# Slots 4 to 7 turned by TensorE, and the first two FFN tiles by whole products

## The chip, the cores and the metric

One core of one Trainium2 chip runs the whole program. The time is device time in microseconds of one execution. The program is one launch: attention for 64 heads, then a feed-forward block over its output, in fp32.

## The reference, cut to what matters

```python
# attention: q, k, v of shape (8, 8, 576, 64), tau = 0.02
scores = scale * q @ k.T
scores = np.where(scores >= max(scores) - tau, scores, -1e9)
attn = np.exp(scores - max(scores))
attn = attn / (np.sum(attn, -1) + 1e-9)
x = (attn @ v) as (8 * 576, 8 * 64)              # 4608 tokens x 512
# FFN: w_in (512, 1024), w_out (1024, 512), g_ln (1024,); the weights come as float64
h = x @ w_in
solu = h * softmax(h)
ln = (solu - mean) / np.sqrt(var + 1e-6) * g_ln
out = ln @ w_out                                 # (4608, 512)
```

## The kernel before, in words

**Slots and rounds.** The work is a list of 144 slots, 18 for each of the 8 batches. A slot `(b, kind, hp, r)` is one 128-row block of scores for two heads: for kinds 0 and 1, `hp` names one of four pairs of heads and `r` one of two row blocks, and slots come in twos (r = 0 and 1) that form a *unit*; the last two slots of a batch (kind 2) gather the 64 rows that are left of every head. A loop goes through rounds, one slot per round, and goes on behind the last slot until the FFN is done. What each engine does in a round is written out by hand (`tc.manual_schedule()`), and every engine works through its own instructions in the order in which the program text issues them. So the order in the text is the order in the queue.

**One slot.** `scores` puts the products of the two heads into two PSUM tiles s0 and s1 (128x576 of 128x1024 each). `maxes` finds each row's threshold on VectorE (L455), `ramp` applies it on ScalarE (L470), `exps` takes the exponentials and their sums on ScalarE (L479). One round later `normalise` forms 1/(sum + 1e-9) on GpSimd (L486, L487) and multiplies both blocks by it there (L489). `blocks` then transposes 32x32 blocks on VectorE (L501), and when both slots of a unit are there, three DMAs (L510, L512) move groups of 32 partitions so that the keys lie on the partitions (tile `wT`). All DMAs but one are issued by SyncE's queue.

**The attention product.** `attend_steps` multiplies a unit's `wT` by v with 64x64 products (L542; an fp32 product is two TensorE instructions, so 72 per unit); `attended` copies the result into the token tile `xh` on ScalarE (L572). The list `pv_due` says in which round a unit's product is due: three rounds behind its second slot, four for some early ones. Products, FFN tiles and other short uses share two PSUM tiles of 128x1024, p0 and p1, which `take` hands out and which return to `pairs_free`.

**The FFN.** A tile of 128 tokens goes through `ff_h` (hidden product in two halves, L605, 64x64 products with a fence in between), `ff_max`, `ff_exp`, `ff_mul`, `ff_sum`, `ff_stats`, `ff_norm` (ScalarE, V), `ff_norm2` (VectorE), `ff_swap` (four DMAs), `ff_turn` (32x32 transposes, L697), `ff_o` (output product, two halves, L710), `ff_out` and `ff_store`. The variables `cur`, `prev` and `quarter` walk through this in quarters, one per round. The first tiles, (0,0,0) and (0,0,1), can begin when the four units of kind 0 of batch 0 have their products.

**The first 16 rounds** also convert the weights from float64 to fp32, one piece of 128x512 per round: `weight_e` on ScalarE (L263), `weight_m` on VectorE (L282 and L286), `weight_b` on VectorE (L308), `weight_c` on GpSimd (L332), and for w_out `weight_f`, a multiplication by the gain on ScalarE (L340). `weight_d` (L347) then copies halves of two pieces of w2 to other partitions by two DMAs. The pieces are loaded by `weight_load` some rounds ahead.

## Time and profile before

| | before |
|---|---|
| median of 3 runs | 860.53 us (854.51 to 861.35) |
| span of the profiled execution | 854.9 us, 36109 instructions |
| TensorE busy, products | 819.9 us (96%) |
| VectorE busy | 674.6 us (79%) |
| ScalarE busy | 570.0 us (67%) |
| GpSimd busy | 496.1 us (58%) |
| DMA, moved | 168.54 MB, 197 GB/s on average |

The profiled execution is one of its own, beside the three runs; the profile gives its span from the first to the last instruction and no other time for it. The span lies 0.4 us above the lowest of the three runs and 5.6 below their median. Busy times count what an engine's instructions take, without its queue's waiting. In rows of the trace the engines are PE (TensorE), PEld (its weight loads), DVE (VectorE), ACT (ScalarE), POOL (GpSimd) and SP (SyncE); a row of the order of time gives the start in us, the length in us, engine, line, operation, what it writes and reads, and how many instructions are joined in it; behind it in brackets stands the idle time ahead and what ended it. A row of a group gives busy us and the mean in ns.

### The profile page before, as it was taken

To read this page: it belongs to the slowest core of one execution; us is meant where nothing else is said; L and a number is where in the kernel's file an instruction comes from. 1 tells how busy PE (TensorE), PEld (TensorE's weight loads), DVE (VectorE), ACT (ScalarE), POOL (GpSimd) and SP (SyncE) were. 2 spreads that over 40 slices of the span, in tenths; PEclk is the share of its full clock that TensorE was granted. 3 is DMA by queue.
4 is the path that set the end of the run, shared out by engine and by line. 5 is a ranking of instruction groups with operands and counts; after the bars stand their busy time and mean duration, and the time that the engine had idled before them with its cause. 6 is when DMAs were issued, how large, how long until landed. Compare 5 with 4: busy or idle time off the path is not lost.

```text
span 854.9 us, 36109 instructions
## 1 busy us (share of the span) xinstructions
PE 819.9 (96%) x15363; PEld 620.5 (73%) x15363; DVE 674.6 (79%) x1225; ACT 570.0 (67%) x1127; POOL 496.1 (58%) x945
## 2 busy tenths in 40 slices
PE   6778899999999999999999999999999999999997
PEld 5555677778677787777688877777777777777655
DVE  5997787989788888888788878888888878787361
ACT  6886876777767666667666666666677777775121
POOL 4885656666566656565566666565666655555120
PEclk8899999999999999999999999999999999999999
DMA  9999778798888888887888778887788887655212
GB/s 343 254 249 213 191 194 233 188 259 204 226 229 202 211 185 218 216 216 190 201 215 218 195 177 209 207 217 207 195 221 226 207 188 175 165 137 140 67 38 63
DMA packets 75314, 168.54 MB, mean 197 GB/s; under 512 B 11146, under 2 KB 32658, under 8 KB 75154
## 3 DMA queue, kind: packets, MB, share of 16 engines
q1 hardware_dynamic: 74866, 165.82, 76.7%
q8 instruction: 120, 1.97, 1.0%
q10 hardware_dynamic: 288, 0.43, 0.2%
q14 instruction: 40, 0.33, 0.1%
HBM read 46.14 MB, written 9.44 MB: 65 GB/s over the span
## 4 chain that ended last, share of the span: by engine, by line
PE 83%; DMA 4%; DVE 4%; ACT 3%; issue 2%; POOL 2%; SPq 1%; DVEq 0%; ACTq 0%; POOLq 0%
PE o_ps L710 27%; PE h_ps L605 22%; PE s_ps L434 15%; PE pv L542 14%; DMA wT<-T 3%; PE h_ps L595 3%; ACT w L470 1%; DVE w L455 1%; ACT w L479 1%; DVE T L501 1%; POOL w L489 1%; POOL sm L487 0%; PE s_ps L379 0%; DVE w L308 0%; PE tp L371 0%
## 5 line engine op out<-in xcount | busy, mean ns | idle before, releaser
L710 PE MATMUL o_ps<-w,uT 64*64 64x256 f32 x4608 | 269.5, 376 | 2.2 <-issue 1.6
L470 ACT ACTIVATE w<-s_ps,nth 128x576 f32<-128x576 f32 x280 | 196.8, 738 | 105.6 <-DVE nth L455 88.6
L455 DVE CUSTOM_DVE_ANT_0 w<-s_ps,tau_t 128x576 f32<-128x576 f32 x280 | 200.0, 751 | 83.5 <-PE s_ps L434 52.4
L710 PEld LDWEIGHTS o_ps<-w,uT 64*64 64x64 f32 x4608 | 221.8, 133 | 55.4 <-ACT xh L572 12.0
L489 POOL TENSOR_SCALAR w<-w,sm 128x576 f32<-128x576 f32 x288 | 220.6, 778 | 14.3
L501 DVE STREAM_TRANSPOSE T<-w 128x576 f32<-128x576 f32 x288 | 207.7, 756 | 22.6 <-POOL w L489 22.3
L605 PE MATMUL h_ps<-w,xh 64*64 64x512 f32 x1856 | 220.8, 589 | 0.0
L479 ACT ACTIVATE w<-w,ntau 128x576 f32<-128x576 f32 x288 | 219.6, 767 | 0.0
L542 PEld LDWEIGHTS pv<-wT,v 64*64 64x64 f32 x5760 | 172.6, 136 | 39.8 <-issue 16.7
L434 PE MATMUL s_ps<-kT,qT 64*64 64x512 f32 (+1 forms) x2048 | 175.8, 416 | 13.4 <-ACT w L470 11.3
L542 PE MATMUL pv<-wT,v 64*64 64x128 f32 (+1 forms) x5760 | 173.9, 263 | 8.3 <-DMA wT<-T 7.4
L605 PEld LDWEIGHTS h_ps<-w,xh 64*64 64x64 f32 x1856 | 118.4, 133 | 77.2 <-issue 43.6
L486 POOL TENSOR_SCALAR sm<-sm 128x2 f32<-128x2 f32 x144 | 34.2, 237 | 186.5 <-ACT w L479 182.8
L487 POOL TENSOR_TENSOR sm<-sm,mone 128x2 f32<-128x2 f32 x144 | 106.7, 741 | 12.0
L434 PEld LDWEIGHTS s_ps<-kT,qT 64*64 64x64 f32 x2048 | 72.7, 137 | 21.7 <-ACT w L470 16.2
L572 ACT COPY xh<-pv 128x256 f32<-128x256 f32 x64 | 25.4, 396 | 80.9 <-PE pv L542 80.9
L671 ACT ACTIVATE V<-u,nb,rs 128x1024 f32<-128x1024 f32 x36 | 44.7, 1240 | 40.5 <-POOL nb L661 33.6
L697 DVE STREAM_TRANSPOSE uT<-V 128x1024 f32<-128x1024 f32 x36 | 44.1, 1225 | 15.9 <-DMA V<-u 15.6
L479 ACT ACTIVATION_READ_ACCUMULATOR w<-w,ntau 128x1 f32 x288 | 55.4, 192 | 0.0
L676 DVE TENSOR_SCALAR u<-u,rs,nb 128x1024 f32<-128x1024 f32 x36 | 34.9, 971 | 19.5 <-ACT V L671 17.9
L635 DVE TENSOR_TENSOR u<-h_ps,u 128x1024 f32<-128x1024 f32 x36 | 42.8, 1190 | 9.4 <-ACT u L629 9.4
L620 DVE TENSOR_REDUCE hm<-h_ps 128x1 f32<-128x1024 f32 x36 | 42.9, 1193 | 4.9 <-PE h_ps L595 2.7
(77 smaller groups left out, 553.5 us busy)
## 6 DMA issues: line engine op xcount, KB each, us to landing
wT<-T SPq DMA_DIRECT2D x160, 288.0 KB, 6.5
wT<-T SPq DMA_DIRECT2D x64, 576.0 KB, 5.5
v<-in_v_dram SPq DMA_DIRECT2D x16, 576.0 KB, 6.0
V<-u SPq DMA_DIRECT2D x144, 64.0 KB, 3.5
out_dram<-ob SPq DMA_DIRECT2D x71, 128.0 KB, 2.6
q<-in_q_dram SPq DMA_DIRECT2D x28, 288.0 KB, 6.1
k<-in_k_dram SPq DMA_DIRECT2D x27, 288.0 KB, 6.4
qT<-flip SPq DMA_DIRECT2D x48, 144.0 KB, 3.2
```

What stands on the lines that cost most here:

```text
L434: nc.tensor.matmul(out=ps[h][ROWS[y], ks], lhsT=lhsT, rhs=d["kT"][ROWS[h], ks], start=True, stop=True,)
L455: nc.vector.tensor_tensor_reduce(out=w, in0=ps[:, 0:S], in1=(zero if loose else tau_t).to_broadcast([P, S]), scale=1.0, scalar=BIG, op0=AL ...
L470: nc.scalar.activation(out=d["w"][x], in_=d["w"][x] if d["loose"] else d["ps"][x][:, 0:S], func=AF.Prelu, bias=d["nth"][x], scale=-1.0, al ...
L479: nc.scalar.activation(out=w, in_=w, func=AF.Exp, bias=ntau, scale=1.0, accum_out=sm[:, x : x + 1])
L487: nc.gpsimd.tensor_tensor(out=sm, in0=sm, in1=mone, op=ALU.pow)
L489: nc.gpsimd.tensor_scalar(out=w, in0=w, scalar1=sm[:, x : x + 1], scalar2=1.0, op0=ALU.mult, op1=ALU.mult)
L501: nc.vector.transpose(out=T[:, :, r, h, :], in_=w)
L542: nc.tensor.matmul(out=to, lhsT=d["v"][ROWS[u], (h0 + h - u) % 4, m,], rhs=rhs, start=m == 0, stop=m == NK - 1,)
L605: mm = nc.tensor.matmul(out=h[ROWS[y], f], lhsT=x[ROWS[r], c, ROWS[y]], rhs=w1_parts[ROWS[r], c, part ^ r], start=part == 0 and c == 0, st ...
L671: nc.scalar.activation(out=V, in_=u, func=AF.Identity, bias=nb, scale=rs)
L697: nc.vector.transpose(out=uT, in_=d["V"].rearrange("p y (m x) -> p m y x", x=32))
L710: nc.tensor.matmul(out=d["o"][ROWS[z], 512 * (r ^ other) : 512 * (r ^ other) + 256], lhsT=d["uT"][ROWS[r], m].rearrange("p y x -> p (y x)" ...
```

## The change

Slots 4 to 7 (two units, kind 0, the third and fourth pair of heads) are no longer turned by VectorE and DMAs. `flip` turns the exponentials by 128x128 transposes on TensorE: four full blocks per head into one PSUM tile (`room`), the last 64 columns into a corner of a second one (`extra`). ScalarE copies the corner (`keep_rest`), VectorE the rest (`keep_flip`). These slots are not multiplied by 1/sum; `attend_flipped` spreads 1/sum over the rows by a product with the identity, ScalarE copies that to SBUF, and `attended_flipped` multiplies behind the product with v. For that v of these heads is loaded in another order (`load_moved_v`), and in batch 0 the keys lie in their natural order.

The inverse of sums is formed on VectorE for slots 4 to 17 and for the FFN in rounds 4 to 17 (`inverse`). The first step of a weight's conversion, L282, goes to GpSimd for pieces 4 and later (`weight_s`), the gain (`weight_f`) from ScalarE to GpSimd, and the copies of `weight_d` to rounds 13, 15, 17 and 19.

A table, `STEPS`, says for rounds 5 to 18 which attention product ("a"), which quarter of a hidden product ("c"), which turning of u ("x") and which half of an output product ("o") TensorE does. The first two FFN tiles use whole 128x128 products and are turned by TensorE (`ff_flip`), so `ff_norm2`, `ff_swap` and `ff_turn` fall away for them. From round 19 on the old walk goes on, with the second tile's output product first in line behind a hidden product.

```diff
+    def load_moved_v(b, hf, parts):
+        d = halves.setdefault((b, hf), dict(moved=True))
+        if 0 in parts:
+            d["v"] = loads.tile([P, 4, NK, D], F32, tag="v", bufs=3, name="v")
+        of = rows_of["v"][64 * (H * b + 4 * hf) :][0:256].rearrange("(h p) (m d) -> p h m d", p=64, d=D)
+        for part in parts:
+            to, which = (
+                (d["v"][ROWS[0], :, 1:NK], of[:, :, 0 : NK - 1]),
+                (d["v"][ROWS[0], :, 0], of[:, :, NK - 1]),
+                (d["v"][ROWS[1]], of),
+            )[part]
+            nc.sync.dma_start(out=to, in_=which)
...
+            of = d.get("scaled", m)
+            if of is m:
+                nc.vector.tensor_scalar(
+                    out=m.bitcast(F32), in0=hi.bitcast(F32), scalar1=2.0**-112, scalar2=None,
+                    op0=ALU.mult,
+                )
...
+    def weight_s(x):
+        if in_bits(x):
+            hi = raws[x]["raw"].bitcast(F32).rearrange("p (n two) -> p n two", two=2)[:, :, 1]
+            dst = piece(x)[1]
+            nc.gpsimd.tensor_scalar(
+                out=dst, in0=hi, scalar1=2.0**-112, scalar2=1.0, op0=ALU.mult, op1=ALU.mult
+            )
+            raws[x]["scaled"] = dst.bitcast(I32)
...
         if wide and x >= 2 * NP:
             _, dst, unit = piece(x)
-            nc.scalar.activation(out=dst, in_=dst, func=AF.Copy, scale=unit)
+            nc.gpsimd.tensor_scalar(
+                out=dst, in0=dst, scalar1=unit, scalar2=1.0, op0=ALU.mult, op1=ALU.mult
+            )
...
+    def inverse(s, sm, power):
+        if FLIP0 <= s < PER:
+            nc.vector.tensor_scalar(out=sm, in0=sm, scalar1=1e-9, scalar2=None, op0=ALU.add)
+            nc.vector.reciprocal(out=sm, in_=sm)
+            return
+        nc.gpsimd.tensor_scalar(out=sm, in0=sm, scalar1=1e-9, scalar2=None, op0=ALU.add)
+        nc.gpsimd.tensor_tensor(out=sm, in0=sm, in1=power, op=ALU.pow)
+
     def normalise(s):
         d = live[s]
         sm = d["sm"]
-        nc.gpsimd.tensor_scalar(out=sm, in0=sm, scalar1=1e-9, scalar2=None, op0=ALU.add)
-        nc.gpsimd.tensor_tensor(out=sm, in0=sm, in1=mone, op=ALU.pow)
+        inverse(s, sm, mone)
+        if FLIP0 <= s < FLIPS:
+            return
...
+    def flip(s, extra):
+        b, kind, hp, r = slots[s]
+        d = live.pop(s)
+        if r == 0:
+            units[b, kind, hp] = dict(
+                wT=work.tile([P, 2, NP, 2, P], F32, tag="wT", bufs=2, name="wT"),
+                more=work.tile([P, 2, 2, 2 * P], F32, tag="T", name="T"),
+                rc=[],
+            )
+        unit = units[b, kind, hp]
+        unit["rc"].append(d["sm"])
+        tag, room = take("flip")
+        rest = extra[ROWS[0], 768:1024]
+        for h, w in enumerate(d["w"]):
+            nc.tensor.transpose(out=rest[:, P * h : P * h + P], in_=w[:, SM:S], identity=ident)
+        for c in range(NP):
+            for h, w in enumerate(d["w"]):
+                x = P * (2 * c + h)
+                nc.tensor.transpose(out=room[:, x : x + P], in_=w[:, P * c : P * c + P], identity=ident)
+
+        def keep_rest():
+            nc.scalar.copy(out=unit["more"][ROWS[0], 0, r], in_=rest)
+
+        def keep_flip():
+            nc.vector.tensor_copy(out=unit["wT"][:, r].rearrange("p c h n -> p (c h n)"), in_=room)
+            pairs_free.append(tag)
+
+        return keep_rest, keep_flip
+
+    def attend_flipped(key):
+        b, kind, hp = key
+        unit = units[key]
+        d, h0 = source(b * NP + hp)
+        if "y" not in unit:
+            unit["y"] = take("pv")
+        y = unit["y"][1]
+        for r in range(2):
+            for h in range(2):
+                nc.tensor.matmul(
+                    out=y[ROWS[h], 512 + P * r : 512 + P * r + P],
+                    lhsT=unit["rc"][r][:, h : h + 1].to_broadcast([P, 64]), rhs=ident,
+                    start=True, stop=True,
+                )
+        nc.scalar.copy(out=unit["more"][:, 1, 0], in_=y[:, 512:768])
+        for c in range(NP + 1):
+            for h in range(2):
+                if c < NP:
+                    lhsT = d["v"][:, h0 + h, 2 * c + 1]
+                    rhs = unit["wT"][:, :, c, h]
+                else:
+                    lhsT = d["v"][ROWS[0], h0 + h, 0]
+                    rhs = unit["more"][ROWS[0], 0, :, P * h : P * h + P]
+                nc.tensor.matmul(
+                    out=y[ROWS[h], 0:256].rearrange("p (r n) -> p r n", r=2), lhsT=lhsT, rhs=rhs,
+                    start=c == 0, stop=c == NP,
+                )
+
+    def attended_flipped(key):
+        b, kind, hp = key
+        unit = units.pop(key)
+        tag, y = unit["y"]
+        to = xh[b, kind][:, hp].rearrange("p (n r) -> p r n", r=2)
+        y, rc = [x.rearrange("p (r n) -> p r n", r=2) for x in (y[:, 0:256], unit["more"][:, 1, 0])]
+        nc.vector.tensor_tensor(out=to, in0=y, in1=rc, op=ALU.mult)
+        pairs_free.append(tag)
...
+        if "y" not in unit:
+            unit["y"] = take("pv")
...
+    def ff_chunk(t, c):
+        x = tokens(t)
+        if c == 0:
+            tag, h = take("h_ps")
+            ffn[t] = dict(h=h, tag=tag)
+        for part in range(2):
+            f = slice(512 * part, 512 * part + 512)
+            nc.tensor.matmul(
+                out=ffn[t]["h"][:, f], lhsT=x[:, c], rhs=w1[:, c, f], start=c == 0, stop=c == NP - 1,
+            )
+
+    def ff_flip(t):
+        d = ffn[t]
+        V = d["V"].rearrange("p g n -> p (g n)")
+        tag, room = take("flip")
+        for c in range(NC):
+            nc.tensor.transpose(out=room[:, P * c : P * c + P], in_=V[:, P * c : P * c + P], identity=ident)
+        d["uT"] = uT = work.tile([P, DFF], F32, tag=TURNED[t], bufs=1, name="uT")
+        nc.scalar.copy(out=uT[:, 0:512], in_=room[:, 0:512])
+        nc.vector.tensor_copy(out=uT[:, 512:DFF], in_=room[:, 512:DFF])
+        pairs_free.append(tag)
+
+    def ff_whole_o(t, part):
+        d = ffn[t]
+        if part == 0:
+            d["otag"], d["o"] = take("o_ps")
+        for c in range(NP * part, NP * part + NP):
+            nc.tensor.matmul(
+                out=d["o"][:, 0:DM], lhsT=d["uT"][:, P * c : P * c + P], rhs=w2[:, 2 * c],
+                start=c == 0, stop=c == NC - 1,
+            )
...
     def ff_sum(t):
-        se = ffn[t]["se"]
-        nc.gpsimd.tensor_scalar(out=se, in0=se, scalar1=1e-9, scalar2=None, op0=ALU.add)
-        nc.gpsimd.tensor_tensor(out=se, in0=se, in1=mone[:, 0:1], op=ALU.pow)
+        inverse(rnd, ffn[t]["se"], mone[:, 0:1])
...
+    FLIP0, FLIPS = 4, 8
+    T0, T1 = (0, 0, 0), (0, 0, 1)
+    STEPS = {
+        5: [("a",)], 7: [("a",)], 8: [("a",)],
+        9: [("c", T0, 0), ("a",)], 10: [("c", T0, 1), ("c", T0, 2)], 11: [("c", T0, 3), ("c", T1, 0)],
+        12: [("c", T1, 1), ("c", T1, 2)], 13: [("a",), ("c", T1, 3)], 14: [("x", T0)], 15: [("a",)],
+        16: [("x", T1), ("o", T0, 0)], 17: [("o", T0, 1), ("a",)], 18: [("a",)],
+    }
+    FREE = max(STEPS) + 1
+    COPIES = {13: 9, 15: 11, 17: 13, 19: 15}
+    TURNED = {T0: "uT", T1: "xh3"}
+    U_HOME = {T1: "xh3"}
 
     pv_due = []
     for s, (b, kind, hp, r) in enumerate(slots):
         if r == 1:
-            pv_due.append((s + LAG_PV + (s < 6 or s in (11, PER - 1, PER + 9)), (b, kind, hp)))
+            pv_due.append((s + LAG_PV + (s in (PER - 1, PER + 9)), (b, kind, hp)))
...
-            if rnd == 13:
-                prev, cur, quarter = cur, None, 0
+            planned = STEPS.get(rnd, [])
+            kinds = [x[0] for x in planned]
+            if rnd == FREE:
+                ready = [(at, ts) for at, ts in ready if ts[0] != T0]
+                prev, cur, quarter = T1, None, 0
             if (
-                cur is None and quarter == 0 and ready and ready[0][0] <= rnd
+                rnd >= FREE and cur is None and quarter == 0 and ready and ready[0][0] <= rnd
...
-                idle = quarter == 0 and cur is None and (
+                idle = not planned if rnd < FREE else quarter == 0 and cur is None and (
...
+            due = rnd >= FREE and bool(pv_due) and pv_due[0][0] <= rnd
+            evict = spare = None
+            if FLIP0 < rnd <= FLIPS:
+                spare, extra = take("pv")
+                keep_rest, evict = flip(rnd - 1, extra)
+                keep_rest()
+            for what, *on in planned:
+                if what == "a":
+                    key = pv_due.pop(0)[1]
+                    if spare is not None:
+                        units[key]["y"] = spare, extra
+                        spare = None
+                    if "rc" in units[key]:
+                        attend_flipped(key)
+                    else:
+                        for _ in attend_steps(key):
+                            pass
+                        attended(key)
+                    if key[1:] == (1, NP - 1):
+                        ready.append((rnd + 1, [(0, 1, 0), (0, 1, 1)]))
+                elif what == "c":
+                    ff_chunk(*on)
+                    if on[1] == NP - 1:
+                        t = on[0]
+                        late.setdefault(rnd, []).append(lambda t=t: (ff_max(t), ff_exp(t)))
+                        late.setdefault(rnd + 1, []).append(lambda t=t: (ff_mul(t), ff_sum(t)))
+                        middle.setdefault(rnd + 2, []).append(lambda t=t: ff_stats(t))
+                        norms[rnd + 3] = t
+                elif what == "x":
+                    ff_flip(*on)
+                else:
+                    ff_whole_o(*on)
+                    if on[1]:
+                        begin.setdefault(rnd + 1, []).append(lambda t=on[0]: ff_whole_out(t))
+                        late.setdefault(rnd + 1, []).append(lambda t=on[0]: ff_whole_store(t))
...
+            if evict is not None:
+                evict()
+            if spare is not None:
+                pairs_free.append(spare)
+            for x in planned:
+                if x[0] == "a" and "rc" in units.get(key, ()):
+                    attended_flipped(key)
             if rnd - 1 in live:
                 blocks(rnd - 1)
...
+            if FLIP0 <= rnd + 3 < NW:
+                weight_s(rnd + 3)
             if rnd - 1 in pieces:
                 weight_f(pieces[rnd - 1])
-                weight_d(pieces[rnd - 1])
                 w2_done = pieces[rnd - 1] == NW - 1
+            if rnd in COPIES:
+                weight_d(COPIES[rnd])
```

70 lines of the change are left out of this document (48 added, 22 removed).

## The prediction

> **What bounds the kernel now.** I read the page first: the busy times, and the 40 slices of 21.4 us each.
>
> ```profile
> span 854.9 us, 36109 instructions
> PE 819.9 (96%) x15363; PEld 620.5 (73%) x15363; DVE 674.6 (79%) x1225; ACT 570.0 (67%) x1127; POOL 496.1 (58%) x945
> ...
> PE   6778899999999999999999999999999999999997
> ...
> DMA  9999778798888888887888778887788887655212
> ```
>
> TensorE has 35 us without work in the whole span, and most of it lies in the first six slices. Behind them the program runs at TensorE's pace. So this change, which touches the first 19 rounds alone, is worth what it does to the moment at which TensorE can begin round 19. For that I cut the start at rounds 5, 10, 13 and 19, which I found in the order of VectorE's instructions (each round begins with two row maxima, L455).
>
> ```profile
> 33.41 0.75 DVE L455 CUSTOM_DVE_ANT_0 w<-s_ps,tau_t 128x576 f32<-128x576 f32 x1
> 56.54 0.75 DVE L455 CUSTOM_DVE_ANT_0 w<-s_ps,tau_t 128x576 f32<-128x576 f32 x1
> 78.37 0.76 DVE L455 CUSTOM_DVE_ANT_0 w<-s_ps,tau_t 128x576 f32<-128x576 f32 x1 [4.86 <-PE s_ps L434]
> 113.55 0.76 DVE L455 CUSTOM_DVE_ANT_0 w<-s_ps,zero 128x576 f32<-128x576 f32 x1
> 110.12 1.45 PE L379 MATMUL s_ps<-ident,k 64*64 64x64 f32 x50
> ```
>
> The busy times of these stretches, with the granted clock and the DMA share as the last but one and last but two figures:
>
> ```profile
> 33.41:56.54 23.13, 16.14 (x296) 10.94 (x289) 22.30 (x46) 19.44 (x41) 19.45 (x27) 0.85 0.99 256
> 56.54:78.37 21.83, 16.65 (x260) 12.26 (x264) 15.59 (x30) 13.56 (x27) 16.52 (x23) 0.92 1.02 235
> 78.37:113.55 35.18, 31.59 (x676) 23.44 (x672) 27.88 (x53) 28.79 (x60) 22.12 (x40) 0.95 0.78 181
> 160.00:800.00 640.00, 636.87 (x12069) 489.22 (x12065) 527.53 (x953) 441.07 (x875) 386.54 (x751) 1.00 0.80 200
> ```
>
> Rounds 5 to 9 take 23.1 us, 4.63 each, and VectorE is busy for 22.3 of them: it is the bound there, TensorE is not (16.1). From 56.5 to 78.4 nobody is: the 16 DMA engines are full, and the chain of waits shows what is late.
>
> ```profile
> 61.22 12.33 DMA wT<-T
> 73.59 3.27 PE pv L542 x65
> ```
>
> The transposed weights of slots 8 and 9 needed 12.3 us to land. From 160 us on TensorE is busy for 636.9 of 640, so a delay at round 19 is not made good later, and a gain isn't lost. One early round of all engines, round 8, is what most terms below come from:
>
> ```profile
> 47.31 0.75 DVE L455 CUSTOM_DVE_ANT_0 w<-s_ps,tau_t 128x576 f32<-128x576 f32 x1
> ...
> 48.06 1.47 POOL L489 TENSOR_SCALAR w<-w,sm 128x576 f32<-128x576 f32 x2
> 48.16 1.42 ACT L470 ACTIVATE w<-s_ps,nth 128x576 f32<-128x576 f32 x2 [0.62 <-DVE nth L455]
> 48.84 1.50 DVE L501 STREAM_TRANSPOSE T<-w 128x576 f32<-128x576 f32 x2
> ...
> 49.64 1.60 PE L434 MATMUL s_ps<-kT,qT 64*64 64x64 f32 x12 [0.35 <-ACT w L470]
> ...
> 50.26 1.05 DVE L308 SCALAR_TENSOR_TENSOR w<-raw,em 128x512 int32<-128x512 int32 x1
> 50.91 0.19 ACT L479 ACTIVATION_READ_ACCUMULATOR w<-w,ntau 128x1 f32 x1
> 51.35 0.43 DVE L282 TENSOR_SCALAR em<-raw 128x512 f32<-128x512 f32 x1
> 51.81 0.43 DVE L286 TENSOR_SCALAR em<-em 128x512 int32<-128x512 int32 x1
> 52.16 0.75 DVE L455 CUSTOM_DVE_ANT_0 w<-s_ps,tau_t 128x576 f32<-128x576 f32 x1
> ```
>
> VectorE does two maxima, two transposes (L501), then three conversions (L308, L282, L286), without a gap. ScalarE's last exponential ends at 51.10, 3.8 us after the first maximum began. All of this hides behind VectorE.
>
> **The change part by part.** *What it takes away.* Two of the eight early units lose their two pairs of VectorE transposes (1.5 us a round) and their three transfers; the multiplications by 1/sum on GpSimd (1.47) go for slots 4 to 7; L282 (0.46 a round) moves to GpSimd. In their place VectorE copies 1024 columns out of PSUM in rounds 5 to 8 (1.1, from L620 below) and forms 1/sum itself: two instructions on 128x2, 0.23 each at the row below, 0.3 together as they overlap.
>
> The trap lies in PSUM. The last copies of the program read two different column ranges of one PSUM tile, o_ps, and one engine waited for the other although nothing overlaps:
>
> ```profile
> 850.36 0.37 ACT L722 COPY ob<-o_ps 128x256 f32<-128x256 f32 x1 [6.32 <-PE o_ps L710]
> 850.76 0.42 DVE L723 COPY ob<-o_ps 128x256 f32<-128x256 f32 x1 [9.56 <-ACT ob L722]
> ```
>
> VectorE stood 9.56 us and began when ScalarE had ended: the program orders any two engines on one PSUM tile, whatever the columns. The new rounds put such pairs in TensorE's queue. In rounds 5 to 8 the last 64 columns are transposed into a corner of the tile `extra`, ScalarE copies this corner out (`keep_rest`), and the attention product of the round goes into the same tile. `keep_rest` stands in ScalarE's queue behind both exponentials of the round, so TensorE, in order, holds the product, and behind it the next round's scores, until then. Before, the next scores ran as soon as the ramp (L470) was through (49.64 above, behind the row of 48.16).
>
> ```profile
> 33.12 2.29 PE L542 MATMUL pv<-wT,v 64*64 64x128 f32 x72 [0.79 <-ACT qT L390]
> 50.81 3.70 PE L542 MATMUL pv<-wT,v 64*64 64x128 f32 x70
> 60.79 1.23 PE L434 MATMUL s_ps<-kT,qT 64*64 64x512 f32 x12
> L572 ACT COPY xh<-pv 128x256 f32<-128x256 f32 x64 | 25.4, 396 | 80.9 <-PE pv L542 80.9
> 106.67 3.63 PE L710 MATMUL o_ps<-w,uT 64*64 64x256 f32 x64
> 115.03 0.23 DVE L462 TENSOR_SCALAR both<-both,tau_t 128x2 f32<-128x2 f32 x1
> ```
>
> *Rounds 5 and 7.* First maximum to last exponential 3.8, copy 0.4 (L572 has 128x256 in 0.396), attention product 2.3 to 3.7, I take 2.6, next scores 1.2, three semaphores 0.2: 8.2 for 4.63 before, +3.6 each, **+7.2**. The ten 128x128 transposes are not in the trace. From below: 64x64 ones pass at 0.03 each (50 in 1.45 us), 0.3 in all; from above: weight load 0.19 (row further down) and a pass of 0.11, with nothing overlapping, 3.0. I take 1.6; they lie in the time in which TensorE waits for the exponentials, and cost nothing while it does. Without that cover they are on its path.
>
> *Round 6* has no product, so the wait falls on nothing: VectorE has 1.4 + 0.3 + 1.1 + 1.5 and some 0.3 of waiting, 4.6, as before.
>
> *Round 8* has the product of the new kind: 3.8 + 0.4, then 1/sum spread over rows by products with the identity (8 instructions of 128 columns, two side by side; four side by side take 0.13 in the 72 of 2.29 us, so 0.5, and 0.1 for the start: 0.6), ScalarE's copy of it 0.4, the product (20 of 256 columns, two side by side; 64 in fours take 3.63, so 2.3), the multiplication on VectorE 0.4, and behind this in VectorE's queue the conversions 1.5; 0.3 of semaphores: 9.7, **+5.1**. What is queued behind the waiting multiplication is the next round's maximum, and for that everybody waits.
>
> *Round 9*: the copy of the spread 1/sum stands behind both exponentials again: 3.8 + 0.4 + 2.3 + 0.4, then transposes of slot 8 1.4, conversions 1.5, gaps 0.3: 10.1, **+5.5**.
>
> A rule differs here from the row. The Trainium skill (PSUM — Partial Sum Buffer, section PSUM bank collisions raise a hardware error) asks only for order between engines on one bank and quadrant, and a bank has 512 fp32 columns. By that the product in columns 0 to 255 need not wait for a copy of columns 512 to 767, round 9 would be some 2.7 us shorter and round 8 0.4, and the sum would be 3.1 lower; the copies above, of columns 0 to 255 and 512 to 767, did wait, so I go by the row.
>
> *Rounds 1 to 4*: GpSimd was busy for 3.9 per round (19.45 of 23.13 over five) and gets 0.65 more (512 columns at the 0.74 that it needs for 576 above): about 4.6 with nothing to spare, level with VectorE. **+0.2**, between 0 and 1.2.
>
> *Rounds 10 to 18* took 57.0 before, the 12.3 us transfer and ScalarE's and TensorE's waits of rounds 15 to 18 included. The transfer has time now (issued in round 10, needed in round 13). VectorE per round: 1.4 maxima, 0.3 for 1/sum, then a new wait: GpSimd's multiplication can only start now, and the first of its two takes 0.74, with the hand-over 0.85; before it ran beside the maxima (48.06 above). Then 1.4 transposes and, to round 13, 1.5 conversions: 5.4. The two FFN tiles add these:
>
> ```profile
> L620 DVE TENSOR_REDUCE hm<-h_ps 128x1 f32<-128x1024 f32 x36 | 42.9, 1193 | 4.9 <-PE h_ps L595 2.7
> L635 DVE TENSOR_TENSOR u<-h_ps,u 128x1024 f32<-128x1024 f32 x36 | 42.8, 1190 | 9.4 <-ACT u L629 9.4
> L650 DVE BATCH_NORM_STATS2 bs<-u 128x6 f32<-128x512 f32 x72 | 46.2, 683 | 0.1
> L671 ACT ACTIVATE V<-u,nb,rs 128x1024 f32<-128x1024 f32 x36 | 44.7, 1240 | 40.5 <-POOL nb L661 33.6
> 85.40 0.96 ACT L388 COPY kT<-s_ps 128x448 f32<-128x448 f32 x2
> L595 PEld LDWEIGHTS h_ps<-w,xh 128*128 128x128 f32 x48 | 8.8, 190 | 11.1 <-issue 10.3 <-DVE T L501 0.8
> 780.72 3.70 PE L595 MATMUL h_ps<-w,xh 128*128 128x512 f32 x8
> ```
>
> Maximum 1.15 in rounds 11 and 13, product 1.1 in 12 and 14, statistics 1.5 in 13 and 15 (0.85 of it in the new wait). Rounds 10 to 13: 21.6 + 4.1 = 25.7. Round 14: ScalarE has V 1.2, the ramps 1.4, copies for the next batch 1.0 and the exponentials 1.6 before its half of the turned u, 0.6, and VectorE's half waits for this one as in the last copies: 5.8 and some 0.2 of semaphores, then on VectorE 0.6 + 1.4 + 1.1 + 0.9, 10.0, of which ScalarE does 0.3 in the round before: 9.7. Round 15: 4.6. Rounds 16 and 17 are TensorE's: scores 2 x 1.0, 0.8 for the next batch, eight transposes 1.5, two halves of a whole output product 2 x 3.5 (8 instructions in 3.70), attention product 2.0, and four changes between 64x64 and whole products 0.8 (an estimate: 8 x 0.43 is 3.4 of the 3.70), 14.1. Round 18: 4.0. Sum 58.1, **+1.1**; with the new waits hidden 8 less, with a colder clock 5 more.
>
> *Round 19.* Eight attention products are done by then and seven before, **-2.0**; TensorE was 3.4 ahead of VectorE there (the rows of 110.12 and 113.55), now 2.6, **+0.8**. The later one-tile output product costs the same either way (7.4 against 7.3). Copies of w2 move from full DMA engines to less full ones; they are needed long after.
>
> Sum: 7.2 + 5.1 + 5.5 + 0.2 + 1.1 - 2.0 + 0.8 = **+17.9**. The profiled execution spans 854.9, 5.6 below the median of the three runs (860.53) and level with the lowest (854.51). So 872.8 for an execution like it, 878.4 at the median's distance from it; I predict **875**, between them. The unknowns (the products' clock, rounds 10 to 18, this distance) make 864 to 886.
>
> **The rivals.** (a) *The transfers were the price, and the waits are not there.* If TensorE needn't wait for ScalarE's copies, rounds 5 to 9 cost TensorE's own work: scores 1.2, transposes 1.6, product 2.6, +0.8 in rounds 5 and 7, some 1.4 each in 8 and 9, +4.4. Rounds 10 to 18 then lose the stall and run near TensorE's own work (scores 9.0, seven chunks of the hidden product 12.0, next batch 3.7, four attention products 8.0, transposes 3.0, output 7.0, mode changes 2.4: 45), say 48, -9.0. With 0.2 - 2.0 + 0.8 it is -5.6: 849.3, and 852 as above between profile and median. It decides as soon as rounds 5 to 9 cost under 8 us. For it speaks the 12.3 us transfer; against it the pair of copies at 850 us.
>
> (b) *Half is made good.* The waits are there, but rounds 10 to 18 have slack in every engine (VectorE's bare work is 9 x 3.1 + 6.9 + 8.6, 43.4): with 50 there, 8 less, and the four products and scores at full clock, 3 less, it is +7: 861.8, and 865 between profile and median. Against it: the order of VectorE's queue.
>
> (c) *The clock falls.* TensorE is idle for half of rounds 5 to 9, and the granted clock was 0.85 there already, with products between 2.29 and 3.70. At 3.70 four products cost 4.4 more, and scores at half the clock 0.9 more in four rounds: 880.8, and 883 between profile and median. A rule points there: the Trainium skill (TensorE: Matmul & The Clock Gate, section Part 4: PE-mode transpose) says that transposes don't count as activity for the clock; no run here shows it yet.
>
> (d) *The transfers stay late* (the change doesn't do what it says): v's second half now has rows of 256 bytes, and slots 8 and 9 wait again, 5 us in round 13: 877.8, and 880.
>
> **How the numbers follow.** Forecast 0.52, (a) 0.16, (b) 0.13, (c) 0.13, (d) 0.06. About 1% (8.6 us) is what a measurement of this kernel can tell from no change. Of (a) 0.10 lies beyond that on the fast side and 0.06 within; (b) lies within; of the forecast 0.05 lies within. Faster 0.10, same 0.24, slower 0.66. The range leaves out most of (a)'s fast part and the ends of (c): 853 to 888.
>
> **What would show it.** Right: maxima of rounds 6, 8, 9 and 10 start some 8, 8, 10 and 10 us after the ones before; products of rounds 5 and 7 are released by ScalarE's copy of `more`; VectorE stands 2 to 4 us before xh<-pv,more; no 12 us transfer at 61 us; TensorE begins round 19 near 130 us. Wrong: products that start right behind the transposes, or round 10 at VectorE before 65 us, or round 19 at TensorE before 112 us.

## The result, and the profile after

| | before | after |
|---|---|---|
| median | 858.86 us (854.51 to 861.35, 4 runs) | 895.66 us (892.30 to 900.23, 4 runs) |
| ratio to before, 95% interval | | 1.045 (1.0395 to 1.0505) |
| span of the profiled execution | 854.9 us | 894.2 us |

The change makes the kernel slower: the medians lie 37 us apart, the ratio is 1.045, and the two profiled executions lie 39.3 apart. The page of the changed kernel, in the same 40 slices (now 22.4 us each; the last row is GB/s), shows where:

```profile
span 894.2 us, 35381 instructions
PE 843.0 (94%) x15011; PEld 609.1 (68%) x15011; DVE 674.3 (75%) x1241; ACT 568.3 (64%) x1125; POOL 488.5 (55%) x923
...
PE   6668789889999999999999999999999999999997
...
PEclk9768889989999999999999999999999999999999
DMA  9930648778886978798788888888788877655312
GB/s 336 236 101 19 188 119 223 169 206 232 216 224 168 241 199 191 205 229 206 193 219 217 215 201 198 211 214 204 189 228 224 207 182 191 164 132 139 74 36 61
```

The DMA engines, full in the first slices of before, do next to nothing in the fourth (19 GB/s). Only a part of that is the transfers that the change removes: rounds 5 to 9 moved 5.9 MB before (23.13 us at 256 GB/s) and now move 4.9 (47.72 us at 103, below), so most of the emptiness comes from the length of these rounds. TensorE isn't busier in these slices, and its granted clock falls to 0.6 in the third. Over the whole program it is busy 843.0 us where it was 819.9, with fewer instructions (15011, 15363 before). The same in the windows of rounds 5 to 9, 10 to 18 and 19 to 31 (columns: length, busy us of PE, PEld, DVE, ACT, POOL, then clock, DMA share, GB/s):

```profile
33.97:81.69 47.72, 34.33 (x326) 20.81 (x327) 21.33 (x50) 20.36 (x44) 13.04 (x15) 0.75 0.39 103
81.69:143.00 61.31, 51.25 (x693) 30.54 (x695) 43.98 (x99) 38.73 (x79) 32.69 (x48) 0.89 0.59 152
143.00:218.40 75.40, 67.79 (x1144) 42.17 (x1140) 54.20 (x104) 47.58 (x97) 41.47 (x80) 0.93 0.82 208
```

Rounds 5 to 9 took 23.1 us and take 47.7, with a granted clock of 0.75. VectorE, the bound before with 22.3 us of work, has 21.3 and stands still for more than half: no engine's work bounds these rounds, the engines wait for each other. The first maxima of rounds 5 to 10 follow each other at 10.5, 4.2, 10.5, 11.7 and 10.9 us:

```profile
33.97 0.74 DVE L488 CUSTOM_DVE_ANT_0 w<-s_ps,tau_t 128x576 f32<-128x576 f32 x1
44.43 0.75 DVE L488 CUSTOM_DVE_ANT_0 w<-s_ps,tau_t 128x576 f32<-128x576 f32 x1
48.66 0.75 DVE L488 CUSTOM_DVE_ANT_0 w<-s_ps,tau_t 128x576 f32<-128x576 f32 x1
59.15 0.75 DVE L488 CUSTOM_DVE_ANT_0 w<-s_ps,tau_t 128x576 f32<-128x576 f32 x1
70.84 0.75 DVE L488 CUSTOM_DVE_ANT_0 w<-s_ps,tau_t 128x576 f32<-128x576 f32 x1
81.69 0.75 DVE L488 CUSTOM_DVE_ANT_0 w<-s_ps,tau_t 128x576 f32<-128x576 f32 x1
```

Who waits for whom, from the orders of time of TensorE and VectorE; the last row is from round 14 (the bracket is the idle time ahead and what ended it):

```profile
38.34 3.79 PE L660 MATMUL pv<-wT,v 64*64 64x128 f32 x72 [3.34 <-ACT T L593]
52.70 4.12 PE L660 MATMUL pv<-wT,v 64*64 64x128 f32 x72 [2.26 <-ACT T L593]
63.18 1.12 PE L610 MATMUL pv<-ident,sm 128*64 128x128 f32 x8 [3.24 <-ACT T L593]
64.77 3.68 PE L624 MATMUL pv<-wT,v 128*64 128x256 f32 x16 [0.47 <-ACT T L615]
74.87 2.93 PE L624 MATMUL pv<-wT,v 128*64 128x256 f32 x16 [2.15 <-ACT T L615]
...
42.16 1.22 DVE L596 COPY wT<-flip 128x1024 f32<-128x1024 f32 x1 [6.14 <-DMA v<-in_v_dram]
56.88 1.22 DVE L596 COPY wT<-flip 128x1024 f32<-128x1024 f32 x1 [6.16 <-PE pv L660]
69.37 0.43 DVE L635 TENSOR_TENSOR xh<-pv,T 128x256 f32<-128x256 f32 x1 [7.05 <-PE pv L624]
78.97 0.43 DVE L635 TENSOR_TENSOR xh<-pv,T 128x256 f32<-128x256 f32 x1 [6.41 <-PE pv L624]
114.14 0.69 DVE L752 COPY uT<-flip 128x512 f32<-128x512 f32 x1 [3.33 <-ACT uT L751]
```

The forecast chain is there: TensorE waits for ScalarE's copy of the corner (L593) or of the spread 1/sum (L615). Behind it is one that was not forecast: in rounds 5 and 7 VectorE's copy of the flipped tile (L596) waits 6.14 and 6.16 us. `wT` has two buffers; units 2 and 3 take those of units 0 and 1, and these are free when the round's own old product ends. The row at 42.16 names a transfer of v as the releaser; its twin at 56.88 names the product, and both copies begin when the product ends.

How far each kernel's round starts behind the one of before (first maximum less first maximum, us) is the measure for all that follows:

| kernel | round 10 | 19 | 25 | 32 | 143 |
|---|---|---|---|---|---|
| changed | 25.1 | 29.5 | 34.5 | 38.2 | 37.9 |
| flips alone | 26.8 | 24.1 | 22.2 | 21.9 | 28.3 |
| walk alone | 2.4 | 11.3 | 16.1 | 17.4 | 20.4 |
| product first | 13.9 | 19.1 | 23.3 | 27.2 | 33.2 |
| VectorE's waits last | 17.4 | 21.9 | 26.9 | 28.9 | 30.5 |
| VectorE's half of u first | 25.6 | 28.2 | 32.7 | 35.4 | 36.6 |
| walk from round 20 | 25.1 | 30.5 | 33.8 | 33.6 | 35.5 |
| ordered | 7.0 | 10.9 | 15.1 | 17.7 | 17.6 |
| ordered, all | 4.7 | 5.7 | 10.8 | 10.5 | 13.1 |
| ordered, copy sooner | 3.2 | 4.2 | 8.6 | 9.7 | 12.6 |
| the same, swap on ScalarE | 2.6 | 4.0 | 5.8 | 9.4 | 9.8 |
| flips ordered, old walk | 2.0 | -0.9 | -2.7 | -2.7 | 0.8 |
| the same, GpSimd relieved | 3.9 | 2.9 | 1.6 | 1.3 | 8.0 |

### The profile page after: what moved, and what is told of

Its sections match the earlier page's. It is cut to its first block, busy times and chain, and to the rows that moved or that the text cites. A ratio compares the mean times of both kernels' runs of the same rounds, so it can differ in the third digit from the quotient of the medians.

```text
span 894.2 us, 35381 instructions
## 1 busy us (share of the span) xinstructions
PE 843.0 (94%) x15011; PEld 609.1 (68%) x15011; DVE 674.3 (75%) x1241; ACT 568.3 (64%) x1125; POOL 488.5 (55%) x923
## 4 chain that ended last, share of the span: by engine, by line
PE 79%; DMA 6%; DVE 5%; POOL 3%; ACT 2%; SPq 2%; issue 2%; DVEq 0%; POOLq 0%; ACTq 0%
PE o_ps L869 25%; PE h_ps L721 21%; PE pv L660 14%; PE s_ps L467 13%; DMA wT<-T 3%; PE h_ps L711 3%; DMA raw<-in_moe_w_in_dram 2%; DVE w L488 2%; PE o_ps L760 1%; POOL w L534 1%; DVE T L549 1%; PE pv L624 1%; ACT w L503 1%; DVE w L337 1%; ACT w L515 1%
## 5 line engine op out<-in xcount | busy, mean ns | idle before, releaser
L869 PE MATMUL o_ps<-w,uT 64*64 64x256 f32 x4352 | 255.2, 379 | 5.9 <-DVE uT L856 3.5
L869 PEld LDWEIGHTS o_ps<-w,uT 64*64 64x64 f32 x4352 | 212.1, 134 | 57.5 <-issue 17.4
L721 PE MATMUL h_ps<-w,xh 64*64 64x512 f32 x1728 | 203.0, 589 | 0.4 <-issue 0.4
L547 DVE STREAM_TRANSPOSE T<-w 128x576 f32<-128x576 f32 x252 | 181.4, 754 | 23.0 <-POOL w L534 19.9
L660 PEld LDWEIGHTS pv<-wT,v 64*64 64x64 f32 x5616 | 164.5, 137 | 45.4 <-issue 18.5
L467 PE MATMUL s_ps<-kT,qT 64*64 64x64 f32 (+1 forms) x2048 | 166.5, 412 | 13.1 <-ACT w L503 10.8
L660 PE MATMUL pv<-wT,v 64*64 64x128 f32 (+1 forms) x5616 | 167.9, 266 | 10.8 <-ACT T L593 5.6
L721 PEld LDWEIGHTS h_ps<-w,xh 64*64 64x64 f32 x1728 | 104.1, 133 | 78.0 <-issue 48.8
L525 POOL TENSOR_TENSOR sm<-sm,mone 128x2 f32<-128x2 f32 x130 | 96.2, 740 | 10.8
L467 PEld LDWEIGHTS s_ps<-kT,qT 64*64 64x64 f32 x2048 | 66.6, 136 | 22.6 <-ACT w L503 15.9
L688 ACT COPY xh<-pv 128x256 f32<-128x256 f32 x62 | 24.6, 397 | 83.4 <-PE pv L660 83.4
L790 ACT ACTIVATE u<-h_ps,hm 128x1024 f32<-128x1024 f32 x36 | 40.1, 1113 | 16.6 <-DVE hm L781 11.7
```

Source lines behind the costliest of these rows:

```text
L467: nc.tensor.matmul(out=ps[h][ROWS[y], ks], lhsT=lhsT, rhs=d["kT"][ROWS[h], ks], start=True, stop=True,)
L525: nc.gpsimd.tensor_tensor(out=sm, in0=sm, in1=power, op=ALU.pow)
L547: nc.vector.transpose(out=T[:, :, r, h, :], in_=w)
L660: nc.tensor.matmul(out=to, lhsT=values(d, u, h0 + h, m), rhs=rhs, start=m == 0, stop=m == NK - 1,)
L721: mm = nc.tensor.matmul(out=h[ROWS[y], f], lhsT=x[ROWS[r], c, ROWS[y]], rhs=w1_parts[ROWS[r], c, part ^ r], start=part == 0 and c == 0, st ...
L869: nc.tensor.matmul(out=d["o"][ROWS[z], 512 * (r ^ other) : 512 * (r ^ other) + 256], lhsT=d["uT"][ROWS[r], m].rearrange("p y x -> p (y x)" ...
```

## The experiments

My theory was that rounds 5 to 9 lose their time in hand-overs, not in work. The rivals: the new FFN walk is the price, or TensorE's low clock is. Each ratio below is to the kernel before as timed beside that run (medians 856.12 to 857.45 us).

**Flips alone.**

```diff
-    STEPS = { ... rounds 5 to 18 ... }
+    STEPS = {5: [("a",)], 7: [("a",)], 8: [("a",)], 9: [("a",)]}
     ... behind round 9 the walk, the weight copies and the inverse as before ...
```

> The flips of slots 4 to 7 with all that belongs to rounds 0 to 9 of the changed kernel, and behind them the FFN walk of the kernel before (split products, swap transfers, copies of the weights where they were). Theory 'hand-overs': the loss is made in rounds 5 to 9, where TensorE, ScalarE and VectorE hand the same PSUM tiles and buffers to each other; round 10 then starts 25 us later than before (81.7), and of that some 5 us come back in the 12.0 us round 12 of before, whose wait for transfers is then over: 876 to 884 us. Rival 'walk': the rounds lose little by themselves and what is lost comes from the new FFN walk around them: 855 to 865 us.

Measured: 886.3 us, ratio 1.0332 (1.0307 to 1.0356), above the 876 to 884 of the theory. Round 10 is as late as with the whole change, and 25.5 of its 26.8 us arise in rounds 5 to 9. By round 13, 4.7 of them come back, as forecast; between rounds 36 and 60 some 6 are lost again, 3.63 of them in a stop of TensorE in round 39 (last section).

**Walk alone.**

```diff
-    FLIP0, FLIPS = 4, 8
+    FLIP0, FLIPS = 99, 99     # slots 4 to 7 by VectorE and DMAs
-        10: [("c", T0, 1), ("c", T0, 2)],
+        10: [("c", T0, 1), ("a",), ("c", T0, 2)],
```

> The new FFN walk alone: whole products of the first two tiles, their u turned by TensorE, the weight copies where the change puts them, 1/sum on VectorE from round 9 on; slots 4 to 7 and the weight steps of the first rounds as before. The attention products of units 2 and 3 stand in rounds 9 and 10. Theory 'hand-overs': rounds 5 to 9 as before, rounds 10 to 18 cost some 4 us more (61.3 against 57.0 us in the changed kernel) and rounds 19 to 42 another 8: 866 to 872 us. Rival 'walk': most of the 37 us, 880 us or more. Rival 'late transfers': what is lost from round 19 on is only a consequence of the 25 us by round 10 meeting the transfers at another moment, and the walk alone is worth nothing: 853 to 860 us.

Measured: 875.99 us, ratio 1.0237 (1.0171 to 1.0303), above what I gave it and below the rival's. The walk costs some 18 us by itself, 9 of them in rounds 10 to 18. Alone, the two make 47 us, together 37. That they overlap by 10 I can explain in part: rounds 13 to 18 took 45.1 us with the walk alone and 41.7 in the change, and the flips alone met that stop of 3.63 us. The rest I can't explain. In the walk alone VectorE stands behind ScalarE too, in rounds 14 and 16 of its order of time:

```profile
93.38 0.69 DVE L750 COPY uT<-flip 128x512 f32<-128x512 f32 x1 [4.08 <-ACT uT L749]
109.69 0.69 DVE L750 COPY uT<-flip 128x512 f32<-128x512 f32 x1 [5.66 <-ACT uT L749]
```

**Product first.** TensorE does the older unit's product ahead of the flips (rounds 5, 7, 8).

```diff
-                keep_rest, evict = flip(rnd - 1, extra)
-                keep_rest()
                 ...attention product...
+                keep_rest, evict = flip(rnd - 1, extra)
+                keep_rest()
```

> In rounds 5, 7 and 8 TensorE does the attention product of the older unit ahead of the flips, everything else is the changed kernel's. Theory 'hand-overs': the product no longer waits for ScalarE's copy of the last 64 keys (3.34, 2.26 and 3.24 us) and the wT buffer is free before VectorE comes to it (waits of 6.14 and 6.16 us): 8 to 12 us by round 10, 884 to 888 us. Rival 'clock': the products stretch because TensorE stands at a low granted clock (3.8 to 4.1 us where 2.6 were taken), and the order changes little: 892 to 896 us.

Measured: 887.85 us, ratio 1.0354 (1.0323 to 1.0385). TensorE's and VectorE's order of time:

```profile
33.80 2.29 PE L660 MATMUL pv<-wT,v 64*64 64x128 f32 x72 [0.95 <-ACT qT L423]
42.80 2.23 PE L660 MATMUL pv<-wT,v 64*64 64x128 f32 x72
52.59 3.68 PE L624 MATMUL pv<-wT,v 128*64 128x256 f32 x16 [4.10 <-ACT T L615]
...
37.34 1.23 DVE L596 COPY wT<-flip 128x1024 f32<-128x1024 f32 x1 [0.89 <-PE flip L590]
58.41 1.23 DVE L596 COPY wT<-flip 128x1024 f32<-128x1024 f32 x1 [8.14 <-PE flip L590]
```

The products of rounds 5 and 7 take 2.29 and 2.23 us where they took 3.79 and 4.12, and these rounds 5.2 and 5.0 where they took 10.5. With the wait the low clock goes too: it is 1.00 from round 5 to 7, where it was 0.73. So the low clock was a consequence of the waits, and in its turn lengthened the products behind them. What is left sits in round 8, where the product now waits 4.10 us for the spread 1/sum.

**VectorE's waits last.** The copy into wT and the multiplication go to the end of VectorE's round.

```diff
-            if evict is not None:
-                evict()
...
             (transposes, weight steps)
+            if evict is not None:
+                evict()
```

> In rounds 5 to 9 VectorE's two instructions that wait for TensorE (the copy of the flipped tile into wT and the multiplication by 1/sum) go behind its transposes and weight steps of the round instead of ahead of them; the rest is the changed kernel's. Theory 'VectorE's queue': what stands behind these waits (6.14, 6.16, 7.05 and 6.41 us) goes ahead, and rounds 5, 7, 8 and 9 lose 2 to 3 us less each: 884 to 889 us. Theory 'TensorE's waits': TensorE's waits for ScalarE's copies end last in each of these rounds, and VectorE only shows them: 893 to 897 us.

Measured: 887.0 us, ratio 1.0346 (1.0321 to 1.037), 7.7 less at round 10. So VectorE's queue is a part of its own: with only TensorE's waits on the path nothing would have come.

**VectorE's half of u first.**

```diff
-        nc.scalar.copy(out=uT[:, 0:512], in_=room[:, 0:512])
         nc.vector.tensor_copy(out=uT[:, 512:DFF], in_=room[:, 512:DFF])
+        nc.scalar.copy(out=uT[:, 0:512], in_=room[:, 0:512])
```

> The changed kernel with one order turned: of the two copies of a turned u out of its PSUM tile (rounds 14 and 16) VectorE's half goes first and ScalarE's half second. Theory 'one tile, one engine at a time': VectorE's half no longer stands 3.33 and 3.20 us behind ScalarE's, which is queued behind both exponentials, and what VectorE has behind it starts 2.2 and 2.5 us earlier: 4 to 5 us less, 890 to 892 us. Rival 'off the path': VectorE catches up in rounds 15 to 18 where it idles anyway, and less than 1.5 us are left: 894 to 896 us.

Measured: 892.97 us, ratio 1.0431 (1.0402 to 1.046), 2.7 under the changed kernel's 895.66 with intervals that overlap, and between the times of theory and rival. VectorE's wait goes from 3.33 to 1.14 us and is now for TensorE; round 32 is 2.8 us earlier.

```profile
112.39 0.69 DVE L751 COPY uT<-flip 128x512 f32<-128x512 f32 x1 [1.14 <-PE flip L749]
```

**Walk from round 20.**

```diff
-    FREE = max(STEPS) + 1
+    FREE = max(STEPS) + 2
```

> The changed kernel with the free walk beginning in round 20 instead of 19, so that from there on each FFN step lies in the same round as in the kernel before. Theory 'SP's queue': the 4.8 us lost in round 24 come from the swap transfer that stands on SP's queue behind a wT transfer waiting for its buffer, since the walk is a round earlier; with the walk a round later the swap comes after it as before: 4 to 8 us less, 888 to 892 us. Rival 'clock': the 64 products of that round took 6.32 us at a low granted clock wherever they lie: 894 to 897 us.

Measured: 893.36 us, ratio 1.0431 (1.0379 to 1.0484). Round 24 takes 6.3 us (5.9 before) and was 10.7; but 3.1 us are lost in round 21, 1.90 of them in a stop of TensorE for which the profile shows no cause. With that, rounds 19 to 31 lose 3.1 us against the kernel before, where the change loses 8.7. The interval of the whole time doesn't tell this kernel from the change. In the changed kernel, round 24 reads like this in the orders of time of SP's queue and VectorE and, for the last row, in the chain that ended last:

```profile
168.71 0.61 SPq L561 DMA_DIRECT2D wT<-T  x1
169.37 2.93 SPq L563 DMA_DIRECT2D wT<-T  x2
172.40 3.45 SPq L846 DMA_DIRECT2D V<-u  x4
...
178.12 1.25 DVE L856 STREAM_TRANSPOSE uT<-V 128x1024 f32<-128x1024 f32 x1 [5.67 <-DMA V<-u]
...
179.51 6.32 PE o_ps L869 x64
```

SP issues nothing between 159.98 and 168.71, when the product of the unit two before ends and frees a `wT` buffer. The swap was ready before that (VectorE's part of it ends at 165.6, ScalarE's before) and stands behind.

**The three orders together.** Product first, the spread 1/sum copied ahead of the exponentials, VectorE's waits last.

```diff
+                if rnd in (8, 9):
+                    spread(pv_due[0][1])     # products with the identity, ScalarE's copy
                 exps(rnd)
```

> The changed kernel with three orders turned in rounds 5 to 9: the older unit's attention product ahead of the flips, the spread 1/sum copied by ScalarE ahead of the round's exponentials, VectorE's copy into wT and its multiplication behind its other work of the round. Nothing is left out. Theory 'hand-overs': rounds 5 to 7 take what they took before, rounds 8 and 9 some 3 and 2 us more than before (the flipped product at a low clock), so round 10 starts some 5 us later than before instead of 25: 872 to 880 us. Rival 'more work': the flips' own instructions (10 flips, two copies of 1.2 and 0.35 us a round) keep 10 us or more even in the best order: 881 to 888 us.

Measured: 876.64 us, ratio 1.0239 (1.0208 to 1.0269). With the same instructions round 10 is 18.1 us earlier than with the change. This is the decisive run: about half of the loss was order (ratio 1.045 with the change, 1.0239 here).

**All remedies.** The three orders, VectorE's half first, the walk from round 20.

```diff
-    FREE = max(STEPS) + 1
+    FREE = max(STEPS) + 2
     ... the three orders, and VectorE's half of u ahead of ScalarE's ...
```

> All three remedies together: the orders of rounds 5 to 9, VectorE's half of u first, the free walk from round 20. If the causes are separate, the gains add: 862 to 872 us. If they stand in for each other (the later walk only absorbs what was lost before it), the time is that of the orders alone, 872 to 880 us. Below 857 us, that is faster than the kernel before, no theory here expects it: the walk alone cost 18 us.

Measured: 872.87 us, ratio 1.0187 (1.0143 to 1.0231). That is just past the 862 to 872 of added gains and inside the 872 to 880 of gains that stand in for each other, and the interval overlaps that of the three orders alone: the run doesn't decide between the two. Round 21 takes 10.5 us in it, 2.08 of them in a stop like the one above.

**Copy sooner.** As ordered, with VectorE's half first, the walk from round 19, and the spread 1/sum copied before the ramps.

```diff
+                if rnd in (8, 9):
+                    spread(pv_due[0][1])
                 maxes(rnd, loose)
-                    spread(pv_due[0][1])
```

> The changed kernel with the three orders of rounds 5 to 9, VectorE's half of u first, and the spread 1/sum copied ahead of the ramps; the free walk begins in round 19 as in the change. Theory 'hand-overs': 2 to 3 us less in rounds 8 and 9 than with the copy ahead of the exponentials and 2 to 3 us from u: 871 to 874 us. Theory 'walk': what is left then, some 15 us over the kernel before, is the walk's (its wait in round 24 and VectorE's 7 us rounds from 10 to 13), and no order in rounds 5 to 9 can take it away; if instead it comes below 865 us, the walk's share was over-read.

Measured: 868.76 us, ratio 1.0144 (1.0093 to 1.0194), less than the 871 to 874 expected. Its rounds 5 to 9, in the same columns as above:

```profile
34.70:59.70 25.00, 22.87 (x315) 13.66 (x307) 21.77 (x49) 20.08 (x44) 13.34 (x14) 1.00 0.71 197
```

25.0 us where the change took 47.7, at full clock. VectorE is busy for 21.8 of them and TensorE for 22.9: the chain that ended last runs through VectorE in rounds 5, 6 and 9 and through TensorE in 7 and most of 8, so neither alone is the bound. In the change the same instructions kept TensorE busy for 34.3 us, 11.5 more, at a clock of 0.75; how much of that lay on the path isn't shown.

**Swap on ScalarE's queue**, for tile (0,1,0) alone, otherwise the kernel just told.

```diff
-                nc.sync.dma_start(
+                (nc.scalar if t == (0, 1, 0) else nc.sync).dma_start(
```

> The kernel with all orders of rounds 5 to 9 and of u mended, and the four swap transfers of one FFN tile, (0,1,0), issued by ScalarE's queue instead of SP's. Theory 'SP's queue': in round 23 these swaps stand behind a wT transfer that waits until the product of the unit two before has freed its buffer; issued elsewhere they start in round 23, VectorE's transpose of V and the output product come in time, and round 24 takes 6 us instead of 10: 4 us less, 864 to 866 us. Rival 'TensorE': round 24 holds a hidden half, an attention product and the end of an output product, and is as long as TensorE needs: 868 to 870 us.

Measured: 866.37 us, ratio 1.0112 (1.0079 to 1.0144), an interval that overlaps that of the kernel just told. Round 24 takes 7.2 us instead of 10.1, so the wait was SP's queue. But round 31 takes 10.7 us instead of 6.5 and gives it back: from round 25 on the chain of waits runs through wT transfers, one behind the other.

```profile
153.32 10.64 DMA wT<-T
163.98 6.84 DMA wT<-T
...
174.53 10.31 DMA wT<-T
```

**Flips ordered, with the old walk.** The mended orders, and behind round 9 the kernel before.

```diff
+    STEPS = {5: [("a",)], 7: [("a",)], 8: [("a",)], 9: [("a",)]}
     ... product first, spread ahead of the maxima and ramps, VectorE's waits last ...
```

> The flips with the FFN walk of before, as in the run of the flips alone, but with the orders of rounds 5 to 9 turned as in the ordered kernel, and the spread 1/sum of rounds 8 and 9 copied by ScalarE ahead of the ramps, so that the flipped product begins some 2 us earlier still. Theory 'order': the 28 us that the flips cost by themselves were nearly all hand-overs; round 10 starts 3 to 5 us later than before and the 12.0 us of round 12 of before give these back, because its transfers are gone: 854 to 862 us. Rival 'a bound of its own': as with the changed kernel some 8 us or more stay, 865 us or more.

Measured: 861.45 us, ratio 1.0047 (1.0013 to 1.0082): 25 us less than the flips alone, half a per cent over the kernel before. Up to round 96 its profiled execution is ahead of before by up to 4.0 us; rounds 111 and 112 lose that again (last section). So, well ordered, the flips bring nothing and cost next to nothing.

**GpSimd relieved**, in that kernel.

```diff
-        if FLIP0 <= s < FLIPS:
+        if FLIP0 <= s < PER:          # inverse of the sums on VectorE
...
+            if x >= 9:                # the gain on ScalarE again
```

> The flips with the old FFN walk and the mended orders, and GpSimd relieved: the inverse of the sums on VectorE up to round 17 as in the changed kernel, and the gain of the last seven pieces on ScalarE as before the change. VectorE waited 1.82, 1.83 and 1.20 us for GpSimd's multiplication in rounds 11, 12 and 13 of the flips with mended orders. Theory 'GpSimd is late next': some 1 us a round in four rounds less, 856 to 859 us, level with the kernel before or just below it (855 to 857). Rival 'the transfers end last': round 12 waits for the weights' and wT's transfers anyway, 860 to 863 us.

Measured: 865.36 us, ratio 1.0106 (1.0068 to 1.0144). That is over the flips ordered, with intervals that overlap, and over what theory and rival gave: my theory fell. VectorE's transposes of round 9, in the flips ordered and in this kernel:

```profile
55.35 1.47 DVE L549 STREAM_TRANSPOSE T<-w 128x576 f32<-128x576 f32 x2
...
57.25 1.50 DVE L552 STREAM_TRANSPOSE T<-w 128x576 f32<-128x576 f32 x2 [0.98 <-POOL w L537]
```

With the inverse on GpSimd the multiplication of round 9 is done while VectorE takes the maxima. With the inverse on VectorE it comes behind the maxima, GpSimd's multiplication behind it, and VectorE waits 0.98 us for what hung on its own work; round 10 is the same with 0.97. In rounds 11 to 13, where GpSimd was late, the wait did fall, from 1.82, 1.83 and 1.20 to 0.97. But round 15 takes 7.33 us instead of 5.59: there ScalarE's gain, which this edit moved back, waits 2.16 us for GpSimd ahead of ScalarE's other work of the round. The edit changed two things, and the share of each isn't shown. No kernel of these beat the one before.

## Why the prediction was wrong, point by point

The direction held, and in rounds 5 to 9 the mechanism; the size was half, and from round 19 on a step of the argument failed. By the terms of the sum, each as start of one round less start of another in the two profiled executions:

| term | predicted | measured |
|---|---|---|
| rounds 0 to 4 | +0.2 | +0.6 |
| rounds 5 to 9 | +17.8 | +24.6 |
| rounds 10 to 18 | +1.1 | +4.3 |
| round 19 and on | -1.2 | +8.5 |
| behind the last maximum | 0 | +1.4 |
| sum | +17.9 | +39.3 |

*Rounds 5 and 7* (8.2 said, 10.5 measured). The products were released by the copy of the corner, as said. Mis-sized was the product at 2.6 us: 3.79 and 4.12 after waits of 3.34 and 2.26. Left out was a step: that VectorE's copy into wT waits for the buffer of the unit whose product is late, so that the conversions and the copy itself stand behind the product. They take 2.3 us from its end to the next round's first maximum, where I had the next scores with 1.2. I had placed that copy ahead of the conversions at 1.1 us and not asked when its target is free.

*Rounds 8 and 9* (9.7 and 10.1 said, 11.7 and 10.9 measured): 3.68 and 2.93 for the 16 wide products, and their four small ones behind, where I had 2.3 for all 20. VectorE stood 7.05 and 6.41 us before its multiplication, not 2 to 4.

*Rounds 10 to 18* (58.1 said, 61.3 measured). The transfer of 12.3 us was gone as said, and round 14's wait behind ScalarE's half of u was there: 3.33 us. VectorE's new wait of 0.85 for GpSimd measured 1.33 in round 10 and 0.95 to 0.97 in rounds 11, 12, 17 and 18; in rounds 13 to 16 other work of VectorE covered it. Against the parts of the sum, rounds 10 to 13 took 27.4 (25.7 said), round 14 9.0 (9.7), round 15 6.2 (4.6), rounds 16 and 17 13.9 (14.1) and round 18 4.8 (4.0).

*Round 19 and on* (-1.2 said, +8.5 measured) is where the prediction's step failed, not only its size. I counted the work that was already done (-2.0), took the free walk, a round earlier, as neutral, and argued that TensorE is full from 160 us on. It had been nearly full in rounds 19 to 31 too, but in the order of before; the row of the kernel before, to be read beside that of 143.00:218.40 above:

```profile
113.55:180.25 66.70, 63.84 (x1294) 48.45 (x1290) 55.17 (x105) 47.68 (x97) 40.26 (x79) 1.00 0.84 218
```

With 150 instructions fewer these rounds take 8.7 us longer: TensorE stands 4.7 us more (7.6 against 2.9), and its busy time is 4.0 longer at a clock of 0.93 instead of 1.00. Steps moved by one round pass other things on SP's queue: in round 24, 4.8 of the 8.7, the swap of tile (0,1,0) came behind a wT transfer that waits for its buffer. Moving the swap to another queue took 2.9 us from round 24, though later waits gave it back, and without the shift by one round only 3.1 of the 8.7 were lost. The other rounds' part isn't traced to single waits.

*The rivals.* (a) and (b), gains in rounds 5 to 18, did not come. (c) came about as worded: the granted clock of rounds 5 to 9 fell from 0.85 to 0.75, the four products grew, and the scores of round 7 took 2.14. Its 17.8 + 4.4 + 3.6 us put 25.8 into rounds 5 to 9, which measured 24.6; that is near in part by luck, since it too lacked the wait for the buffer, and scores grew once and not four times. Behind round 9 it had nothing more than the forecast, so its 880.8 lies 13.4 under the profiled 894.2. The waits came first: mended, the same rounds run at 1.00. The Trainium skill (TensorE: Matmul & The Clock Gate, section Part 4: PE-mode transpose) says that a transpose doesn't count as busy for the clock in the same way; in the mended kernel the same ten transposes in each of rounds 5 to 8 did no harm. (d) did not happen: round 12, 12.0 us before, took 7.0.

*The rule that I weighed.* The Trainium skill (PSUM — Partial Sum Buffer, section PSUM bank collisions raise a hardware error) asks for order within one bank and quadrant only. Rounds 8 and 9 waited 0.47 and 2.15 us for a copy of other columns, 2.6 of the 3.1 that hung on it, so the row was the better guide: the order is the program's, for the whole tile. The row itself had left another reading open, since its two copies also write one tile, `ob`; the 16 wide products share no tile with the copy that they waited for but that of PSUM.

## What to carry to other kernels

Of a step moved to another engine, ask where it stands in that engine's queue, who else touches its PSUM tile and when its target buffer is free: the same instructions took 47.7 or 25.0 us in these five rounds. Of two users of one tile, the one that isn't late goes first, and a small copy that others wait for goes ahead of long work of its engine. A walk that shifts by one round has to be followed on the DMA queue too, past every transfer that can wait.

## What the runs showed of the hardware

The clock of TensorE is no smooth function of the wait just ahead. The 16 wide products took 1.95 us after a wait of 1.98 (all remedies) and 3.58 after 2.63 (ordered), but also 1.95 after 2.72 (product first, round 9).

```profile
49.87 1.95 PE L627 MATMUL pv<-wT,v 128*64 128x256 f32 x16 [1.98 <-ACT T L612]
...
50.60 3.58 PE L627 MATMUL pv<-wT,v 128*64 128x256 f32 x16 [2.63 <-ACT T L612]
...
65.04 1.95 PE L624 MATMUL pv<-wT,v 128*64 128x256 f32 x16 [2.72 <-ACT T L615]
```

Each of the 14 kernels has one to three places at which TensorE stops for 1.05 to 3.63 us with nothing shown that it waits for. The places go with the program: counted in the traces, a stop lies behind 7086 to 7089 TensorE products (matmul instructions) in six of the kernels with the new walk (0.91 to 2.23 us), and behind 3651 to 3653 in the three with the flips and the old walk (1.00 to 3.63). In two kernels stops follow each other at a distance of 1782 products. In the flips ordered one is in round 112, between two score products, and 32 hidden products behind it take 5.13 us (31 take 3.31 in round 19 of the changed kernel). The second row is from the chain that ended last:

```profile
611.29 1.09 PE L467 MATMUL s_ps<-kT,qT 64*64 64x512 f32 x8 [2.01 <-issue]
...
612.38 5.13 PE h_ps L724 x32
```

Such a stop moves a comparison of two profiled executions by some 2 to 4 us, beside what the edit does itself. Its cause stays open.
